# Token loads of the bonus on ScalarE's DMA queue instead of SyncE's

## The chip, the cores and the metric

One core of one Trainium2 chip. The metric is the time of one execution on the device in microseconds. The kernel before took 586.46 us, the median of three runs (584.77, 586.46 and 588.16).

A core has engines that each run their own instructions strictly in order and wait for one another by semaphores: TensorE (PE, matrix products), VectorE (DVE), ScalarE (ACT), GpSimd (POOL) and SyncE (SP). SyncE computes nothing here; it issues transfers between DRAM and on-chip memory. ScalarE can issue transfers too, from a queue of its own, but an issue is then an instruction among its computations: while ScalarE issues, or waits to issue, its next copy doesn't start.

## The reference

A recurrent attention block feeds a two-layer network. For each of 4 batches and 8 heads, with 768 tokens and 48 channels per head:

```python
for t in range(S):
    cur = einsum('bhd,bhe->bhde', u[None] * kt, vt)
    y[:, :, t] = einsum('bhd,bhde->bhe', rt, state + cur)
    state = wt[:, :, :, None] * state + einsum('bhd,bhe->bhde', kt, vt)
```

The 3072 outputs of 384 channels then go through the network:

```python
h = x @ w_in                        # 384 -> 2048
g = h * (1.0 / (1.0 + np.exp(-h)))  # silu
return g @ w_out                    # 2048 -> 384
```

The term with `u` is the bonus: a token sees itself with the weight `u` in place of the state's decay.

## The kernel before

**Tiling.** The tokens are worked through in 12 units: 6 stretches of 128 tokens, each for two pairs of batches (`units`). In a unit the recurrence is written as a matrix of scores between tokens, built level by level (blocks of 2, 4, ... 64 tokens), where VectorE and GpSimd multiply decays into queries and keys and TensorE forms the products. Scores times values gives the attention's output.

**Staging.** `mix(i)` is the list of steps of unit i's attention. It is a list of groups, and each group comes with a number: so many steps of the network are issued behind it. These steps belong to earlier units: `downs(i - 2)`, the second layer of unit i-2 in 7 steps, then `ups(i - 1)`, the first layer of unit i-1. From unit 3 on the first layer has 20 steps (`first_part`): each is a group of products on TensorE, and between them ScalarE and VectorE copy, join and activate partial sums that stand in four banks. TensorE can go on with a bank only when such a copy or join (L1161 and L1164 on ScalarE, L1167 on VectorE) is done with it. The order is written out by hand: what is issued earlier in this list stands earlier on its engine.

**The bonus from unit 4 on.** `load_rk(i)` loads unit i's r, k and w as tokens (384 KB each) into `tokens_rk` and `tokens_w`, 16 tokens of one head to a row. There is one buffer of each, so a load has to wait until GpSimd has read the unit before. GpSimd makes products from them: `block_bonus(i, 0)` to `(i, 3)` (L490) at the end of unit i-1's mix, and steps 4 to 7 in unit i's own. `tokens_w` is read last in step 5, `tokens_rk` in step 7. VectorE sums the products into `block_sums` (`block_sum`, L527). The sums stand by head and block and are wanted by token, so `block_move` sends them through DRAM: one store to `kept` (L549), and when it has landed, five reads into `spare` (one at L554, four at L556). VectorE turns them (`block_turn`, L560) and writes them into the scores (`block_write`, L566).

**Around the change.** SyncE issues nearly everything, in program order: the blocks of w, k and r for the next unit (L127), its values v (L140, L147), the output stores (L1297), then the r and k tokens (L158), the store of the sums, the w tokens, and the five reads. ScalarE issues only the passage of the attention's output through DRAM (`x_out` L930, `x_in` L936). Behind the group with `block_move` stand, in VectorE's order, joins of the first layer, then `block_turn`, the first half of `block_write`, another join (L1167) and the second half. Each transfer also waits for the one that used the same completion counter before it; there are eight counters in rotation over both queues, in the program's order.

`sum_steps(i, 3)` and `sum_steps(i, 4)` are the last two parts of the sums; `keep_level` and `go_on` belong to the scores; `in_weight_sum` makes sums of weights once, in unit 4. `ahead` is true while there is a next unit, so the token loads stand in mix(4) to mix(10).

Of the kernel before, what the change touches and what calls it, by code (L numbers as in the profile page):

```python
# [38 lines left out]
def kernel(  # L39
# [11 lines left out]
    nc = tc.nc  # L51
# [56 lines left out]
    def load_twos(to, src, i, queues):  # L108
        n, b0 = units[i]
        for b in range(NB):  # L110
            queues[b].dma_start(out=to[b * L // 2:(b + 1) * L // 2],
                                in_=src[b0 + b, :, n * L:(n + 1) * L, :].rearrange("h (i s) d -> i h (s d)", s=2))
# [33 lines left out]
            t1 = t0 + L - (g + 1) * 32  # L146
            nc.sync.dma_start(out=vq[i][g * 32:(g + 1) * 32], in_=v[b0 + 1, :, t1:t1 + 32, :].rearrange("h t d -> t h d"))  # L147

    def load_rk(i, parts=range(3)):

        if i < NPAIR:
            for x, src in enumerate((r, k)):
                load_twos(tokens_rk[:, x].rearrange("p h s d -> p h (s d)"), src, i, [nc.sync] * NB)
            return
        n, b0 = units[i]
        for x in parts:
            to, src = ((tokens_rk[:, 0], r), (tokens_rk[:, 1], k), (tokens_w, w))[x]
            nc.sync.dma_start(out=to.rearrange("p h s d -> p (h s d)"),  # L158
                              in_=src[b0:b0 + NB, :, n * L:(n + 1) * L, :].rearrange("b h (i s) d -> (b h) i (s d)", s=2 * BLK))


# [294 lines left out]
    at = 768  # L456
# [486 lines left out]
    def both(fn, i, *args):  # L943
        return [(fn, i, b, *args) for b in range(NB)]

    def block_loads(i, names="wkr"):
        return [(load_blocks, i, name, g) for name in names for g in range(4)]

    def mix(i):

        ahead = i + 1 < len(units)

        def at(now, *steps):
            return steps if now else ()

        def bonus_steps(j, *steps):
            return [(block_bonus, j, x) for x in steps]

        def sum_steps(j, *steps):
            return [(block_sum, j, x) for x in steps]  # L960

        def turns(j):
            return [*both(turn, j, "w"), (product, j, 0), *both(turn, j, "k")]

        def start(j):
            return [*[(product, j, l) for l in range(1, NL)], (grow_own, j, 1)]

        end = [[*at(ahead, *bonus_steps(i + 1, 0, 1, 2, 3))],
               [*at(i < len(units) - NB, (turn_apart, i), (turn_k, i)), (y_state, i), *both(y_values, i), *at(ahead, *turns(i + 1)), *at(ahead and i > NFAST, *sum_steps(i + 1, 0, 1)),
                *at(i <= NFAST, (sums, i - 1, FH // 2 - 2)), *both(update, i), *at(not ahead, (move_x, i))]]  # L970
        if i < NPAIR:
            groups = [[*both(turn, i, "w"), (product, i, 0)],
                      [*both(turn, i, "k"), (odd_ones, i)], [*both(turn, i, "r"), (start_levels, i), (prepare_keys, i, 1)],
                      [(prepare, i, 1), *[(product, i, l) for l in range(1, NL)]],
                      [(burst, i, 1), (keep_level, i, 1)],
                      [(keep_level, i, 2), (go_on, i, 2)],
                      [(prepare, i, 3), (reverse_v, i), (bonus, i, 0), (bonus_sum, i, 0)],
                      [(bonus, i, 1), (burst, i, 3), (keep_level, i, 3), (bonus, i, 2)],
                      [(keep_level, i, 4), (go_on, i, 4), (bonus_sum, i, 1), (load_rk, i + 1), (load_u,)],
                      [(prepare, i, 5), (make_block_mask,), (bonus_spread, i)],  # L980
                      [(burst, i, 5), (keep_level, i, 5, 0), (keep_level, i, 6, 0), (go_on, i, 6), (bonus_write, i, (0,)), (keep_level, i, 5, 1), (keep_level, i, 6, 1), (bonus_write, i, (1,))], *end]
            groups = list(zip(groups, (1, 1, 0, 2, 1, 1, 1, 1, 1, 2, 2, 1, 1)))
        else:
            j = i - 1
            groups = [([*both(turn, i, "r"), (grow_own, i, 0), (x_out, j)], 2),
                      ([*start(i), *bonus_steps(i, 4), (x_in, j), (reverse_v, i)], 1),
                      ([(grow_queries, i, 2), (sums_of_x, j, 0)], 1),
                      ([(odd_keys, i, 2), (grow_keys, i, 2, False), (sums_of_x, j, 1)], 1),
                      ([(sums_of_x, j, 2), *sum_steps(i, 2), (prepare, i, 3), *bonus_steps(i, 5, 6, 7), (sums_of_x, j, 3, 4, 5, 6)], 2),
                      ([(burst, i, 3), (keep_level, i, 3)], 2),  # L990
                      ([*sum_steps(i, 3)], 1),
                      ([], 1),
                      ([*at(ahead, (load_rk, i + 1, (0, 1))), *sum_steps(i, 4), (block_move, i, False), *at(ahead, (load_rk, i + 1, (2,))), (block_move, i, True), (keep_level, i, 4)], 2),
                      ([(go_on, i, 4)], 1),
                      ([], 2),
                      ([], 1),
                      ([(sums_of_x, j, 7)], 1),
                      ([(prepare, i, 5)], 2),
                      ([], 1),
                      ([(burst, i, 5), (keep_level, i, 5, 0), (keep_level, i, 6, 0), (go_on, i, 6), (block_turn, i), (block_write, i, 1)], 2),  # L1000
                      ([(keep_level, i, 5, 1), (keep_level, i, 6, 1)], 1),
                      ([(block_write, i, 0)], 1),
                      (end[0], 2), (end[1], 0)]

        if i == NPAIR:
            groups[0][0][:0] = sum_steps(i, 0, 1)
        loads = [*at(i >= NPAIR and ahead, *block_loads(i + 1, "wk")), *at(i >= NPAIR - 1 and ahead, *block_loads(i + 1, "r"))]
        if i + 1 < len(units):
            loads.insert(len(loads) // 2, (load_values, i + 1))

        if i < NPAIR:
            behind = [group for group, _ in groups[8:]]
            for at, group in enumerate(behind):
                group += loads[at * len(loads) // len(behind):(at + 1) * len(loads) // len(behind)]
        elif ahead:
            blocks = block_loads(i + 1, "wkr")
            for at, some in ((0, blocks[0:3]), (1, blocks[3:6]), (2, [*blocks[6:8]]), (3, [(load_values, i + 1)]),
                             (9, blocks[8:9]), (10, blocks[9:10]), (11, blocks[10:11]), (12, blocks[11:])):
                groups[at][0].extend(some)
        return groups  # L1020
# [278 lines left out]
    def ups(i):  # L1299

        if i >= NFAST:
            made = [[(first_part, i, n)] for n in ORDER]
            if i == len(units) - 1:
                made[10].append((sums_of_x, i, 7))
            made[17].append((sums, i, 0))
            made[-1].append((sums, i, 1))
            return made
        steps = [[(up, i, m)] for m in range(FC // 2)]
        for m in range(FH // 2 - (1 if i == len(units) - 1 else 2)):

            steps[FH // 2 + 1 + m].append((sums, i, m))
        steps[-1].append((sums, i, FH // 2 - 1))
        return steps

    def downs(i):
        return [[(quarter, i, x)] for x in range(7)]
# [73 lines left out]
    for i in range(3, len(units)):  # L1390
        steps = downs(i - 2) + ups(i - 1)
        groups = mix(i)
        if i == NTOK + 1:
            groups[4][0].insert(1, (weight_sums, 3))
            for place, engine, names in ((4, nc.vector, ("m",)), (5, nc.vector, ("n",)), (6, nc.vector, ("m1", "m2")), (7, nc.gpsimd, ("q14", "q3")),
                                         (8, nc.vector, ("q12a", "q12")), (11, nc.gpsimd, ("q", "n13", "t"))):
                groups[place][0].append((in_weight_sum, engine, *names))
        if i == NFAST + 1:
            keep_banks()
            for place, engine, names in ((4, nc.vector, ("u1",)), (5, nc.vector, ("u",)), (7, nc.vector, ("q19",)), (5, nc.gpsimd, ("q7",)),  # L1400
                                         (8, nc.gpsimd, ("q8", "q1")), (9, nc.gpsimd, ("q5", "q9")), (13, nc.gpsimd, ("q6", "q17"))):
                groups[place][0].append((in_weight_sum, engine, *names))
        for group, count in groups:
            do(*group)
            for step in steps[:count]:
                do(*step)
            steps = steps[count:]
# [34 lines left out]
```

## Time and profile before

| | |
|---|---|
| Median of the runs | 586.46 us |
| The profiled execution | 587.88 us |
| Its span in the profile | 586.0 us |
| TensorE busy | 564.1 us (96%) |
| VectorE busy | 470.4 us (80%) |
| GpSimd busy | 385.3 us (66%) |
| ScalarE busy | 259.6 us (44%) |
| Granted TensorE clock, mean | 0.985 |
| SyncE's queue (q1) | 49.52 MB, 42.0% of the 16 DMA engines' time |
| ScalarE's queue (q10) | 6.88 MB, 4.6% |

How to read the profile: the span runs from the first to the last recorded instruction; the execution's own time lies a little over it. Busy time is the sum of an engine's computing instructions; issues of transfers are not counted in it and stand as SPq (SyncE's) or ACTq (ScalarE's). A line of a timeline gives the start in us from the span's start, the length, the engine, the source line, what is written and read, and in brackets how long the engine was idle before and what ended that. The chain is the work that ended last, followed back from the end; `DMA kept<-block_sums` in it is the time from issue to landing of that transfer. PEclk is the share of full clock that TensorE was granted.

### The profile page before, as it was taken

To read this page: it belongs to the slowest core of one execution; us is meant where nothing else is said; L and a number is where in the kernel's file an instruction comes from. 1 tells how busy PE (TensorE), PEld (TensorE's weight loads), DVE (VectorE), ACT (ScalarE), POOL (GpSimd) and SP (SyncE) were. 2 spreads that over 40 slices of the span, in tenths; PEclk is the share of its full clock that TensorE was granted. 3 is DMA by queue.
4 is the path that set the end of the run, shared out by engine and by line. 5 is a ranking of instruction groups with operands and counts; after the bars stand their busy time and mean duration, and the time that the engine had idled before them with its cause. 6 is when DMAs were issued, how large, how long until landed. Compare 5 with 4: busy or idle time off the path is not lost.

```text
span 586.0 us, 18814 instructions
## 1 busy us (share of the span) xinstructions
PE 564.1 (96%) x7782; PEld 523.5 (89%) x7782; DVE 470.4 (80%) x748; ACT 259.6 (44%) x556; POOL 385.3 (66%) x459
## 2 busy tenths in 40 slices
PE   8989999999999899979999989999999989999997
PEld 7768876798899899969999979999989989999997
DVE  7979789898899999767799879689889879682350
ACT  5679694431531561442372352263263253372330
POOL 6989778457799988747776856765975964810000
PEclk9989999999999999989999998999999999999999
DMA  9957785443445634635634545554455453102000
GB/s 226 314 118 217 161 238 83 48 93 91 95 83 88 134 53 69 151 39 92 138 54 85 113 81 89 103 93 80 81 114 94 88 107 67 34 8 55 29 3 26
DMA packets 206485, 57.59 MB, mean 98 GB/s; under 512 B 186048, under 2 KB 198208, under 8 KB 206400
## 3 DMA queue, kind: packets, MB, share of 16 engines
q1 hardware_dynamic: 198288, 49.52, 42.0%
q10 hardware_dynamic: 8112, 6.88, 4.6%
q8 instruction: 61, 1.00, 0.7%
q14 instruction: 24, 0.20, 0.1%
HBM read 47.14 MB, written 9.18 MB: 96 GB/s over the span
## 4 chain that ended last, share of the span: by engine, by line
PE 47%; DMA 5%; SPq 3%; issue 1%; DVE 1%; POOL 1%; ACT 0%; DVEq 0%
PE p_o L1283 22%; PE p_o L1140 9%; PE p_h L1140 6%; PE p_h L1283 4%; DMA kept<-block_sums 3%; PE p_m L861 2%; DMA spare<-kept 2%; SPq L556 2%; PE p_m L840 2%; PE p_sc L697 1%; PE p_m L697 1%; SPq L158 1%; PE p_sc L906 1%; POOL ruk L490 1%; PE p_sc L816 1%
## 5 line engine op out<-in xcount | busy, mean ns | idle before, releaser
L639 POOL TENSOR_TENSOR tk<-tk,tw 128x256 f32<-128x256 f32 x128 | 96.0, 770 | 45.0 <-ACT tk L609 29.0
L1283 PE MATMUL p_o<-own,temps 128*128 128x192 f32 x528 | 88.1, 326 | 0.2 <-DVE temps L1254 0.2
L1283 PEld LDWEIGHTS p_o<-own,temps 128*128 128x128 f32 x528 | 86.0, 190 | 0.5 <-DVE temps L1254 0.5
L1140 PE MATMUL p_o<-xt,w_in_sb 128*64 128x128 f32 x1152 | 73.9, 274 | 11.1 <-DVE p_o L1167 9.4
L407 POOL TENSOR_TENSOR tw<-tw 128x256 f32<-128x256 f32 (+6 forms) x83 | 41.7, 502 | 55.9 <-DVE tw L361 52.0
L1140 PEld LDWEIGHTS p_o<-xt,w_in_sb 128*64 128x64 f32 x1152 | 64.9, 137 | 12.9 <-DVE p_o L1167 10.8
L1033 PE MATMUL p_h<-xt,w_in_sb 128*128 128x256 f32 x288 | 67.8, 391 | 0.8 <-POOL w_in_sb L260 0.6
L1033 PEld LDWEIGHTS p_h<-xt,w_in_sb 128*128 128x128 f32 x288 | 54.7, 194 | 9.4 <-POOL w_in_sb L260 1.1
L1283 PE MATMUL p_o<-w_out_sb,gt 128*128 128x192 f32 x340 | 60.0, 329 | 1.6 <-DVE ob L1291 0.9
L1283 PEld LDWEIGHTS p_o<-w_out_sb,gt 128*128 128x128 f32 x340 | 55.3, 190 | 2.8 <-DVE ob L1291 1.2
L490 POOL TENSOR_TENSOR ruk<-tokens_rk 128x384 f32<-128x384 f32 x48 | 53.0, 1126 | 4.6 <-DMA tokens_rk<-in_k_dram 4.0
L621 DVE TENSOR_TENSOR tr<-tr,tw 128x512 f32<-128x512 f32 x61 | 54.2, 889 | 0.5
L1288 ACT COPY partial<-p_o 128x192 f32<-128x192 f32 x33 | 10.5, 319 | 93.8 <-PE p_o L1283 80.3
L609 ACT COPY tk<-tk 128x256 f32<-128x256 f32 x52 | 20.9, 402 | 54.8 <-POOL tk L639 40.7
L1254 DVE TENSOR_TENSOR temps<-gt 128x512 f32<-128x512 f32 (+1 forms) x48 | 38.4, 838 | 0.0
L1164 ACT ACTIVATE gt<-p_o 128x512 f32<-128x512 f32 x45 | 26.0, 601 | 24.7 <-PE p_o L1140 24.7
L715 DVE COPY_PREDICATED score<-mask,p_sc 128x512 f32<-128x512 int8 x42 | 31.3, 801 | 3.5 <-PE p_sc L697 3.3
L1283 PE MATMUL p_o<-w_out_sb,temps 128*128 128x192 f32 x176 | 30.4, 326 | 0.0
L797 ACT COPY score<-p_sc 32x128 f32<-32x128 f32 x80 | 20.5, 257 | 20.2 <-DVE score L566 18.2
L1283 PE MATMUL p_h<-w_out_sb,gt 128*128 128x192 f32 x168 | 29.1, 326 | 0.0
L1283 PEld LDWEIGHTS p_o<-w_out_sb,temps 128*128 128x128 f32 x176 | 28.9, 190 | 0.0
L490 POOL TENSOR_TENSOR spare<-tokens_rk 128x384 f32<-128x384 f32 x24 | 28.2, 1188 | 0.6
(239 smaller groups left out, 1273.0 us busy)
## 6 DMA issues: line engine op xcount, KB each, us to landing
w_out_sb<-in_moe_w_in_dram SPq DMA_DIRECT2D x6, 768.0 KB, 7.1
w_out_sb<-in_moe_w_out_dram SPq DMA_DIRECT2D x4, 768.0 KB, 6.7
own<-in_moe_w_out_dram SPq DMA_DIRECT2D x4, 768.0 KB, 5.9
tokens_rk<-in_r_dram SPq DMA_DIRECT2D x8, 384.0 KB, 4.6
tokens_rk<-in_k_dram SPq DMA_DIRECT2D x8, 384.0 KB, 5.4
tokens_w<-in_w_dram SPq DMA_DIRECT2D x8, 384.0 KB, 5.4
turned<-yt ACTq DMA_DIRECT2D x16, 192.0 KB, 2.7
xt<-turned ACTq DMA_DIRECT2D x8, 384.0 KB, 3.8
```

Of the source, the lines that this page charges most:

```text
L407: engine.tensor_tensor(out=up, in0=t[:, :, 0::2], in1=t[:, :, 1::2], op=ALU.mult)
L490: mul = lambda out, one, two: nc.gpsimd.tensor_tensor(out=out, in0=one, in1=two, op=ALU.mult)
L609: nc.scalar.copy(out=keys(i, X[(l + 1) % 2] * L + c, [4 * c, blocks], [c, 2], [1, c]), in_=keys(i, NP * L + c, [4 * c, blocks], [NP * L + ...
L621: nc.vector.tensor_tensor(out=odd, in0=odd, in1=tw[i][l][:, :, 0::2][:, :, :, None].to_broadcast([128, Q, L >> (l + 1), c]), op=ALU.mult)
L639: nc.gpsimd.tensor_tensor(out=out, in0=have, in1=odd_products(i, l, b, *blocks), op=ALU.mult)
L715: nc.vector.copy_predicated(out=dst, mask=masks[l][:, :, None].to_broadcast([128, NB, NP, ni, c]), data=sc[e].rearrange("p (b q) (i c) -> ...
L797: nc.scalar.copy(out=score[x * c:(x + 1) * c, i % NSC, e, b * NP:(b + 1) * NP, (first + 1) * c:(first + 2) * c], in_=made[i, l][e][x * c:( ...
L1033: nc.tensor.matmul(p_h[:, a, :], lhsT=w_in_sb[:, c, f * 128:(f + 1) * 128], rhs=xt[i][:, c, :], start=(a == 0 and c == 0), stop=(a == 1 an ...
L1140: nc.tensor.matmul(p[h:h + PD, q, :], lhsT=left[:, f:f + PD], rhs=right, start=first and q == 0, stop=q == 3, skip_group_check=True)
L1164: nc.scalar.activation(out=g(f, t), in_=have, func=AF.Silu)
L1254: nc.vector.tensor_tensor(out=out, in0=one, in1=two, op=op)
L1283: nc.tensor.matmul(p, lhsT=left(f), rhs=right[:, f, :], start=which in (0, 1, 3) and f == 0, stop=f == FH - 1, skip_group_check=True)
```

## The change

The r, k and w tokens of the next unit are issued from ScalarE's queue in place of SyncE's, in mix(4) to mix(10). `load_rk` takes the queue as an argument. The w load is taken out of `block_move`'s middle and put one group ahead, in a group that was empty; the r and k loads are taken out of the head of the same group and put three groups later: the empty group of two steps behind `go_on` is cut into two of one step each, and they stand in the second. The numbers of steps behind the groups are the same in sum. As there is one group more, the weight sums that were put into group 13 go into group 14, the same place as before. Block loads that are put into groups by number (9 to 12) stand one step of the network earlier for two of the r blocks.

In the built programs the order on TensorE, VectorE and GpSimd is the same in both. SyncE has 21 issues fewer. ScalarE has 21 more, at two places in each of the seven mixes: w behind the second of two copies at L1161 and ahead of an activation (L1164); r and k behind an activation at L1183 and ahead of a copy at L1161.

```diff
-    def load_rk(i, parts=range(3)):
+    def load_rk(i, parts=range(3), queue=nc.sync):
...
-            nc.sync.dma_start(out=to.rearrange("p h s d -> p (h s d)"),
+            queue.dma_start(out=to.rearrange("p h s d -> p (h s d)"),
                               in_=src[b0:b0 + NB, :, n * L:(n + 1) * L, :].rearrange("b h (i s) d -> (b h) i (s d)", s=2 * BLK))
...
                       ([*sum_steps(i, 3)], 1),
+                      ([*at(ahead, (load_rk, i + 1, (2,), nc.scalar))], 1),
+                      ([*sum_steps(i, 4), (block_move, i, False), (block_move, i, True), (keep_level, i, 4)], 2),
+                      ([(go_on, i, 4)], 1),
                       ([], 1),
-                      ([*at(ahead, (load_rk, i + 1, (0, 1))), *sum_steps(i, 4), (block_move, i, False), *at(ahead, (load_rk, i + 1, (2,))), (block_move, i, True), (keep_level, i, 4)], 2),
-                      ([(go_on, i, 4)], 1),
-                      ([], 2),
+                      ([*at(ahead, (load_rk, i + 1, (0, 1), nc.scalar))], 1),
                       ([], 1),
                       ([(sums_of_x, j, 7)], 1),
...
-                                         (8, nc.gpsimd, ("q8", "q1")), (9, nc.gpsimd, ("q5", "q9")), (13, nc.gpsimd, ("q6", "q17"))):
+                                         (8, nc.gpsimd, ("q8", "q1")), (9, nc.gpsimd, ("q5", "q9")), (14, nc.gpsimd, ("q6", "q17"))):
```

## The prediction

> **What bounds the kernel now.** I read the page's chain first, then the busy time by stage, then the chain in order of time at one stage, then the SyncE, ScalarE and VectorE rows there. Times written as +x are us after TensorE starts the level-3 scores (L697) of a unit; that start is the left edge of each window below, from mix(5) to mix(10).
>
> ```profile
> PE 47%; DMA 5%; SPq 3%; issue 1%; DVE 1%; POOL 1%; ACT 0%; DVEq 0%
> PE p_o L1283 22%; PE p_o L1140 9%; PE p_h L1140 6%; PE p_h L1283 4%; DMA kept<-block_sums 3%; PE p_m L861 2%; DMA spare<-kept 2%; SPq L556 2%; PE p_m L840 2%; PE p_sc L697 1%; PE p_m L697 1%; SPq L158 1%; PE p_sc L906 1%; POOL ruk L490 1%; PE p_sc L816 1%
> ```
>
> TensorE carries the chain, but the trip of the bonus through DRAM (`kept`, then back into `spare`) and its issues stand in it too. By stage:
>
> ```profile
> core 0: us, PE busy (x) PEld busy (x) DVE busy (x) ACT busy (x) POOL busy (x), PEclk, DMA share, GB/s
> 234.90:284.13 49.23, 45.52 (x660) 43.85 (x662) 37.43 (x64) 18.25 (x42) 33.17 (x45) 0.93 0.50 91
> 284.13:326.76 42.63, 42.63 (x693) 41.53 (x695) 37.97 (x59) 18.60 (x43) 29.25 (x35) 1.00 0.48 92
> 326.76:375.43 48.67, 45.75 (x692) 44.47 (x695) 38.15 (x63) 18.65 (x43) 32.93 (x45) 0.93 0.49 89
> 375.43:418.05 42.62, 42.62 (x692) 41.52 (x695) 37.96 (x59) 18.60 (x43) 29.24 (x35) 1.00 0.50 94
> 418.05:461.70 43.65, 42.65 (x693) 41.52 (x694) 38.42 (x63) 18.59 (x43) 32.36 (x41) 1.00 0.51 96
> 461.70:505.09 43.39, 41.55 (x645) 40.37 (x647) 34.62 (x59) 17.99 (x41) 30.71 (x39) 1.00 0.39 80
> ```
>
> Mixes 6 and 8 are gapless: 42.6 us, TensorE busy throughout. Mixes 5 and 7 do the same work in 49.23 and 48.67 and lose clock (0.93); mixes 9 and 10 lose 1.00 and 1.84. The chain in order of time inside mix(7):
>
> ```profile
> 334.81 5.08 DMA kept<-block_sums
> 339.91 0.38 SPq L554
> ...
> 342.73 3.31 DMA spare<-kept
> 346.20 0.24 DVE spare L560
> ...
> 348.01 0.70 DVE p_o L1167
> 348.76 1.09 PE p_o L1140 x16
> ```
>
> Store, five reads back, `block_turn` on VectorE, and behind that wait on the same engine the join of the first layer (L1167), for which TensorE stands still: 3.64, 2.92, 1.00 and 1.84 us in mixes 5, 7, 9, 10. After the two longest the clock is down for a while; after the two short ones it is not:
>
> ```profile
> 299.00:310.00 11.00, 11.00 (x232) 1.00 0.28 42
> 348.00:359.00 11.00, 10.24 (x156) 0.69 0.39 63
> 438.00:449.00 11.00, 10.87 (x179) 1.00 0.46 72
> ```
>
> Why the store takes long: in mix(7) it is issued right behind 768 KB of r and k on the same queue (issues at 333.53, 334.13, store at 334.81) and lands after 5.08; in mix(11), with no token loads, the same store takes 1.55:
>
> ```profile
> 511.52 0.33 SPq L549 DMA_DIRECT2D kept<-block_sums  x1
> 513.07 0.38 SPq L554 DMA_DIRECT2D spare<-kept  x1
> ```
>
> **The change, part by part.** Seven mixes (4 to 10) are touched, 21 loads; mix(11) has none, and units up to 4 are still loaded by SyncE.
>
> *Removed from SyncE.* r (0.55) and k (0.59) ahead of the store, w (0.54) behind it. Sums stand ready at 242.29, 333.93, 425.22 and 468.11 in mixes 5, 7, 9, 10; SyncE is past its two output stores at 242.84, 333.44, 423.96, 467.32. So the store is issued at about 242.90, 333.95, 425.24, 468.13 in place of 244.22, 334.81, 426.21, 468.70: 1.32, 0.86, 0.97 and 0.57 sooner. Its landing was 5.9, 5.1, 4.5 and 5.0. Bounds now: 1.5 (mix 11, no load near) to 5.9. I take 2.3, mix(8)'s, where the store came 3.1 us after k's issue: the w load will stand 2.1 us before it and is half as large. The store then lands near +9.5.
>
> *Added on ScalarE.* An issue occupies the queue in order. Its places in mix(9):
>
> ```profile
> 421.96 0.59 ACT L1161 COPY gt<-p_o 128x512 f32<-128x512 f32 x1 [0.29 <-PE p_o L1140]
> 424.58 0.60 ACT L1164 ACTIVATE gt<-p_o 128x512 f32<-128x512 f32 x1 [2.03 <-PE p_o L1140]
> ...
> 426.33 0.60 ACT L1183 ACTIVATE gt<-p_h 128x512 f32<-128x512 f32 x1 [0.26 <-PE p_h L1140]
> 428.13 0.59 ACT L1161 COPY gt<-p_o 128x512 f32<-128x512 f32 x1 [1.21 <-PE p_o L1140]
> ```
>
> w goes into the 2.03 us hole (0.54 of it): free. r and k (1.14 and some 0.05 between) go into the 1.21 hole: 0 to 0.1 late. If issues run to SyncE's longest, 0.92 and 1.27, the copy behind is 1.0 late; its result is wanted by the join at 429.55 and its bank by the matmuls at 429.50, 0.8 after it now ends. I take 0; upper bound 0.2 x 7 = 1.4 us. What could hold these issues: GpSimd's last reading (w: done 420.24; r and k: 424.22, issue at 426.95), and in the built program a load eight places earlier that shares a completion counter: for w a late k block (issued by 418, landing in 1.9 to 3.5), for r and k loads of v issued by 422.98, landing in 2.7. All are done at least 1 us before.
>
> *The reads back.* Five issues, then a landing: 5.1 us (mix 9) to 6.3 (mix 7), so the blocks are in at +14.6 to +15.8. VectorE comes to them at +16.35 in mixes 7, 9 and 10. But r and k now fly from +8.9 on, beside the reads. Bound from below 0; from above 3.6, what r and k did to the store (5.08 against 1.55). Nearest: mix(8), where w went out 1.9 us before the first read, and the reads' landings were 2.8 to 3.8 against 1.9 to 3.0 in mix(9): 0.9 from 384 KB. For twice as much I take 1.8 at the front, less for the last read, which is issued near +12.6: some 1.0. So +15.6 to +16.8: VectorE waits 0 to 0.45, and TensorE's stall was 0.1 to 0.8 less than that wait in three of four mixes. I put 0.4 us of stall to each of mixes 5 to 10, bounds 0 and 2.
>
> *Moved later: tokens for GpSimd.* k lands 4.2 to 6.1 after its issue near +9.5, so at +13.7 to +15.6; GpSimd starts the next unit's products at +13.84 (431.89). It slips up to 1.8 us. Cover: after those products it waits 9.39, 5.77, 9.35, 5.77, 6.38, 7.57 us for VectorE's `tw` (mixes 5 to 10). Free; without that cover it would cost 1.8 per unit. SyncE reaches its r blocks up to 3.4 us earlier and then waits for VectorE as before.
>
> *Sum.* Stall and lost clock over the gapless length: 49.23 - 42.63 = 6.6; 48.67 - 42.63 = 6.0; 1.0; 1.84: 15.5 us. Less 6 x 0.4 = 2.4: 13.1. That the gapless pace holds from mix to mix is read from mix(9), which follows a gapless one: its sums were ready only 0.8 us later than mix(8)'s. The profiled execution took 587.88 (span 586.0 and 1.88 around it), 1.42 over the median of 586.46. 587.88 - 13.1 = 574.8; as a median, 573.4.
>
> **Rivals.** *Only the issue time is saved.* The reads lose beside r and k what the store wins. Then the stalls shrink by 1.32 + 0.86 + 0.97 + 0.57 = 3.7: 582.7. Stalls of 2.3 and 2.1 remain in mixes 5 and 7, between 1.84, which kept the clock, and 2.92, which did not; if the clock holds, 3.0 + 3.1 more come back: 576.6. For it: r and k fly at the time of the reads. Against it: the last read goes out 3 us after k. The Trainium skill has this as a rule (DMA: Bandwidth & Descriptors, "Issuing engines are not separate DMA queues"): loads started by ScalarE and SyncE run on the same 16 engines and interleave, so a second issuer saves issue time only. By it the time is 582.7 to 576.6; but here the loads also move in time, away from the store, which the rule leaves open. On the clock the Trainium skill (TensorE: Matmul & The Clock Gate, "What's actually happening") halves it after about 3.4 us idle, by which stalls of 2.3 and 2.1 would keep it and the time be 576.6; mix(7)'s 2.92 was already enough, so the trace is less kind.
>
> *Slower: the reads are hit as the store was.* If r and k cost the last read 3.6, it lands at +18.2 to +19.4, VectorE waits 1.9 to 3.0 in mixes 5 to 10, and near 2.9 a stall costs 6.0 with its clock. Six times 6.0 less 15.5 is +20.5: 607. It decides from 15.5 / 6 = 2.6 us lost per mix, so about where the clock starts to fall. Against it: in mix(6) w went out 2.1 us before the reads and they landed in 1.8 to 2.5, not slowed at all.
>
> *Same: the stall is replaced.* ScalarE's copy comes late by two long issues, or a wait of r or k for the loads of v runs over; 15.5 / 7 = 2.2 us per mix would cancel the gain. The v loads would have to land 3 us later.
>
> **How the numbers follow.** As computed (570 to 577): 0.55. Issue time only (577 to 583): 0.24. Replaced, within 0.5% (583.5 to 589.4, about what a measurement of this kernel can tell from no change): 0.08. Slower: 0.13. The first two end faster: 0.79. The range runs from all 15.5 us won, 586.46 - 15.5 = 571.0 less half the runs' spread (1.7), so 569.3, to the end of the issue-only case, 583: 0.79 of the chances.
>
> **What would show it.** Right: three loads per unit at L158 on ScalarE's queue, 0.54 to 0.6 us each; store to landing below 3 us in mixes 5, 7, 9, 10; TensorE's idle time ahead of L1140 for L1167 from 11.1 us to 3 or less; clock 1.00 in the stages that had 0.93; GpSimd waiting for `tokens_rk` up to 1.8 us per mix. Wrong: VectorE still waiting over 2 us at L560 for `spare<-kept`, a copy at L1161 late behind its issues, or a GpSimd that reaches `tw` after VectorE.

## The result and the profile after

The changed kernel takes 580.26 us (median of five runs, 579.7 to 581.95) against 586.46 (five runs, 584.77 to 588.16): a ratio of 0.9895, 95% interval 0.9867 to 0.9923. It is faster by 6.2 us. The forecast was 13.1: its sign was right and its range holds the time, but it was more than twice the gain. The profiled execution took 580.03 (span 578.1, mean clock 1.000 in place of 0.985).

The page's chain of the changed kernel is followed back over only 12% of the span, nearly all of it TensorE. That stretch lies behind mix 10, the last one that was changed, so the view says nothing of the change. (Below the change, line numbers are higher by one than in the kernel before: the join is L1168, the copy L1162, the first layer L1141.) The busy time by stage does say something. The windows run from the first level-3 scores of mixes 5 to 10 to those of the next unit, here in the changed kernel:

```profile
core 0: us, PE busy (x) PEld busy (x) DVE busy (x) ACT busy (x) POOL busy (x), PEclk, DMA share, GB/s
234.66:278.53 43.87, 43.11 (x690) 41.59 (x689) 39.24 (x62) 18.64 (x44) 32.35 (x41) 1.00 0.53 96
278.53:323.97 45.44, 43.23 (x689) 41.57 (x689) 38.87 (x63) 18.53 (x43) 32.58 (x41) 1.00 0.53 94
323.97:366.67 42.70, 42.66 (x689) 41.52 (x689) 38.08 (x60) 18.61 (x43) 31.67 (x39) 1.00 0.51 95
366.67:410.21 43.54, 43.25 (x690) 41.58 (x689) 39.21 (x62) 18.54 (x43) 32.35 (x40) 1.00 0.52 97
410.21:454.76 44.55, 43.25 (x690) 41.57 (x689) 39.05 (x63) 18.54 (x43) 32.79 (x41) 1.00 0.51 94
454.76:496.34 41.58, 41.54 (x641) 40.36 (x641) 35.45 (x57) 17.78 (x41) 30.13 (x36) 1.00 0.42 85
sum 261.68, PE 257.03 PEld 248.20 DVE 229.90 ACT 110.62 POOL 191.87; mean PE 42.84 PEld 41.37 DVE 38.32 ACT 18.44 POOL 31.98
```

and mix 5 and the sum over the same six mixes in the kernel before:

```profile
233.93:284.06 50.13, 46.18 (x689) 44.38 (x688) 38.33 (x65) 18.68 (x44) 34.07 (x47) 0.93 0.50 90
...
sum 271.09, PE 261.38 PEld 253.78 DVE 225.52 ACT 111.11 POOL 188.56; mean PE 43.56 PEld 42.30 DVE 37.59 ACT 18.52 POOL 31.43
```

The two long mixes are gone (43.87 and 42.70 in place of 50.13 and 48.67), and so is the lost clock. But mixes 6 and 8, gapless before at 42.6, now take 45.44 and 43.54, and mix 9 takes 0.9 more than it did. The six mixes give back 9.4 us; the time up to mix 5 and that behind mix 10 are 0.7 and 0.8 longer, which leaves 7.9 between the two spans. The profiled execution of before lay 1.42 above its median, the new one 0.23 below, which makes 6.2 of it.

The waits of the changed kernel (us in total, times, longest):

```profile
ACT gt L1162 <- DMA out_dram<-temps: 8.0, 3, 3.0
DVE spare L560 <- DMA spare<-kept: 7.0, 6, 2.2
PEld p_o L1141 <- DVE p_o L1168: 5.8, 11, 1.6
...
PEld p_o L1141 <- ACT gt L1162: 2.1, 3, 1.1
```

Before, VectorE waited at L560 for 10.7 us in four mixes, and TensorE 11.1 us for the join. Now VectorE waits 7.0 in all six, and there is a wait that did not exist: ScalarE's copy, three times, 2.4 to 3.0 us, each time behind a token load that could not be issued. Before, ScalarE stood idle for 1.2 us ahead of the same copy anyway, until TensorE was done, so the copy comes 1.2 to 1.9 us late. In mix 8, ScalarE's rows of the changed kernel (start, length, engine, line; in brackets the idle time before and what ended it):

```profile
375.53 0.54 ACTq L158 DMA_DIRECT2D tokens_rk<-in_r_dram  x1
377.84 0.54 ACTq L158 DMA_DIRECT2D tokens_rk<-in_k_dram  x1
378.48 0.59 ACT L1162 COPY gt<-p_o 128x512 f32<-128x512 f32 x1 [2.44 <-DMA out_dram<-temps]
```

and SyncE's in the same mix:

```profile
374.89 0.41 SPq L549 DMA_DIRECT2D kept<-block_sums  x1
378.85 0.38 SPq L554 DMA_DIRECT2D spare<-kept  x1
```

r goes out, k waits 1.77 us, and the copy starts 3.03 us after the activation ahead of it (L1184, at 375.45). Before, this distance was 1.80 (in mix 9, 426.33 to 428.13), so the copy is 1.2 late. The store took 3.96 us from issue to the first read, where in the kernel before this mix had 2.31.

### The profile page after: what moved, and what is told of

Read it like the earlier page. It is cut to its first block, busy times and chain, and to the rows that moved or that the text cites. A ratio compares the mean times of both kernels' runs of the same rounds, so it can differ in the third digit from the quotient of the medians.

```text
span 578.1 us, 18816 instructions
## 1 busy us (share of the span) xinstructions
PE 559.5 (97%) x7782; PEld 517.7 (90%) x7782; DVE 477.9 (83%) x748; ACT 259.2 (45%) x556; POOL 389.3 (67%) x459
## 3 DMA queue, kind: packets, MB, share of 16 engines
q10 hardware_dynamic: 11136, 15.14, 10.1%
## 5 line engine op out<-in xcount | busy, mean ns | idle before, releaser
L639 POOL TENSOR_TENSOR tk<-tk,tw 128x256 f32<-128x256 f32 x128 | 94.6, 759 | 36.2 <-ACT tk L609 28.6
L1141 PE MATMUL p_o<-xt,w_in_sb 128*64 128x128 f32 x1152 | 73.6, 274 | 5.8 <-DVE p_o L1168 2.7
L1141 PEld LDWEIGHTS p_o<-xt,w_in_sb 128*64 128x64 f32 x1152 | 64.3, 137 | 8.4 <-DVE p_o L1168 4.3
L1034 PE MATMUL p_h<-xt,w_in_sb 128*128 128x256 f32 x288 | 66.1, 384 | 1.8 <-POOL w_in_sb L260 1.6
L621 DVE TENSOR_TENSOR tr<-tr,tw 128x512 f32<-128x512 f32 x61 | 50.5, 829 | 0.5
L1255 DVE TENSOR_TENSOR temps<-gt 128x512 f32<-128x512 f32 (+1 forms) x48 | 44.1, 956 | 0.0
L648 POOL TENSOR_TENSOR tk<-tk,tw 128x256 f32<-128x256 f32 x32 | 28.1, 898 | 0.0
```

What stands on the lines that cost most here:

```text
L621: nc.vector.tensor_tensor(out=odd, in0=odd, in1=tw[i][l][:, :, 0::2][:, :, :, None].to_broadcast([128, Q, L >> (l + 1), c]), op=ALU.mult)
L639: nc.gpsimd.tensor_tensor(out=out, in0=have, in1=odd_products(i, l, b, *blocks), op=ALU.mult)
L648: nc.gpsimd.tensor_tensor(out=have, in0=have, in1=odd_products(i, l, b, [2, NP * ni]), op=ALU.mult)
L1034: nc.tensor.matmul(p_h[:, a, :], lhsT=w_in_sb[:, c, f * 128:(f + 1) * 128], rhs=xt[i][:, c, :], start=(a == 0 and c == 0), stop=(a == 1 an ...
L1141: nc.tensor.matmul(p[h:h + PD, q, :], lhsT=left[:, f:f + PD], rhs=right, start=first and q == 0, stop=q == 3, skip_group_check=True)
L1255: nc.vector.tensor_tensor(out=out, in0=one, in1=two, op=op)
```

## The experiments

Three theories were on record. A: what is left is traffic, the tokens' bytes beside the small transfers. B: the gapless pace isn't reached anyway, so 15.5 us were never there. C: ScalarE's issues and their waits cost the time. Each ratio is to the kernel before on the same chip.

**e1: no token loads.** From the changed kernel, mixes 4 to 10:

```diff
-                      ([*at(ahead, (load_rk, i + 1, (2,), nc.scalar))], 1),
+                      ([], 1),
...
-                      ([*at(ahead, (load_rk, i + 1, (0, 1), nc.scalar))], 1),
+                      ([], 1),
```

> The changed kernel without the 21 token loads of mixes 4 to 10 (the bonus of units 5 to 11 is computed from old tokens, all else is as before). Theory A (traffic): the token loads slow the transfers that fly beside them, and that is all that is left to win. Then every mix from 5 to 10 takes 41.6 to 42.8 us, VectorE never waits at L560 for the reads, and the time is 571 to 573. Theory B (pace): the gapless 42.6 us of mixes 6 and 8 were a gift of the slow mixes before them, GpSimd can't hold them, and without any token load the time stays at 577 or above, with GpSimd late at the sums.

Measured: 572.38 us against 587.76, ratio 0.9726 (0.9667 to 0.9784). By stage, mix 8 and the sum over the six mixes:

```profile
362.55:405.17 42.62, 42.62 (x690) 41.52 (x689) 38.91 (x61) 18.61 (x43) 32.02 (x40) 1.00 0.43 72
...
sum 255.47, PE 255.09 PEld 248.06 DVE 231.68 ACT 111.08 POOL 192.17; mean PE 42.52 PEld 41.34 DVE 38.61 ACT 18.51 POOL 32.03
```

Mixes 6 to 10 are gapless, and VectorE never waits at L560. (Mix 5 takes 43.49, more than the 42.8 that was expected.) B falls: 15.4 us were to be had, and the loads are the cause of all of it. The changed kernel's mixes are 261.68 - 255.47 = 6.2 us above this.

**e2: w left out. e3: r and k left out.** One of the two lines above is emptied, the other stays.

> The changed kernel without the 7 loads of w (steps 3 and 5 of the bonus use old w). Theory A: w flies beside the loads of v; without it v lands in 3 us or less, so neither the store nor the issues of r and k have to wait for v's completion counters, the store lands in 2.5 us or less, but the reads back stay at 4 us beside r and k. VectorE still waits 0.2 to 1 us per mix; 575 to 577. Theory C (ScalarE held): all that matters is that ScalarE is held by its issues of r and k (0.84 + 0.23 + 0.28 us of TensorE's time); 578.9, and the store lands as late as with w.

> The changed kernel without the 14 loads of r and k (the bonus of units 5 to 11 is computed from old r and k). Theory A: the reads back land in 2 to 3 us in place of 4 to 5, VectorE's wait at L560 (7.0 us in all) goes to under 1.5, the store stays at 2.5 to 4.4; 573 to 576. Theory C: only ScalarE's being held goes, 1.4 us: 578.9, and the reads stay at 4 us.

Measured: e2 577.67, ratio 0.9809 (0.9747 to 0.9872); e3 574.21, ratio 0.9748 (0.9677 to 0.9819). e3 is in A's range. e2 lies between A's 575 to 577 and C's 578.9, so its time decides nothing; that its store lands in 1.9 us, and not as late as with w, is A's. The landings (KB each, median us from issue to landing, mixes 5 to 11, of those that the trace records; each trace lacks some; the 32 KB row is the first read, the 8 KB row the four behind it), first in the kernel before:

```profile
vq<-in_v_dram SPq DMA_DIRECT2D x24, 48.0 KB, 2.5
kept<-block_sums SPq DMA_DIRECT2D x7, 64.0 KB, 4.8
spare<-kept SPq DMA_DIRECT2D x27, 8.0 KB, 2.8
spare<-kept SPq DMA_DIRECT2D x7, 32.0 KB, 2.6
```

the changed kernel:

```profile
vq<-in_v_dram SPq DMA_DIRECT2D x24, 48.0 KB, 4.4
kept<-block_sums SPq DMA_DIRECT2D x7, 64.0 KB, 3.6
spare<-kept SPq DMA_DIRECT2D x28, 8.0 KB, 3.9
spare<-kept SPq DMA_DIRECT2D x7, 32.0 KB, 4.4
```

e2, without w:

```profile
vq<-in_v_dram SPq DMA_DIRECT2D x24, 48.0 KB, 2.4
kept<-block_sums SPq DMA_DIRECT2D x7, 64.0 KB, 1.9
spare<-kept SPq DMA_DIRECT2D x28, 8.0 KB, 4.8
spare<-kept SPq DMA_DIRECT2D x7, 32.0 KB, 5.1
```

e3, without r and k:

```profile
vq<-in_v_dram SPq DMA_DIRECT2D x24, 48.0 KB, 4.1
kept<-block_sums SPq DMA_DIRECT2D x7, 64.0 KB, 3.6
spare<-kept SPq DMA_DIRECT2D x28, 8.0 KB, 2.7
spare<-kept SPq DMA_DIRECT2D x7, 32.0 KB, 2.4
```

The two loads do two separate things. w, moved ahead, flies beside the v loads and the store: 2.4 to 4.4 and 1.9 to 3.6. r and k fly beside the reads: 2.4 to 4.4 or more for the first, 2.7 to 3.9 or more for the others. With w gone ScalarE is no longer held at its copy (no such wait in e2), so C's wait is a consequence of w's traffic: the loads of v land later, and what stands behind them in the rotation of completion counters can't be issued. The waits view names `out_dram<-temps` as the releaser; the built program puts a load of v eight places ahead of k. The two land at about the same time, and no run tells which it was. SyncE is held in the same way: in mixes 5 and 6 its own waits show 0.5 and 1.6 us at the store (L549) for `vt<-in_v_dram`, another load of v, and the store goes out 1.5 and 2.0 us after the sums are ready.

Why bytes matter so much is read from the share of the 16 DMA engines' time (next to last column). The store's flight and the reads' flight in mix 7 of the kernel before:

```profile
336.50:339.90 3.40, 3.40 (x68) 3.40 (x64) 2.97 (x6) 2.11 (x5) 0.46 (x1) 1.00 1.03 268
339.91:344.00 4.09, 4.09 (x120) 3.85 (x118) 2.76 (x3) 3.31 (x9) 4.09 (x6) 1.00 0.30 25
```

and in mix 8 of the changed kernel:

```profile
374.89:378.85 3.96, 3.96 (x74) 3.76 (x70) 3.96 (x7) 1.26 (x3) 1.22 (x3) 1.00 1.05 301
378.85:382.67 3.82, 3.59 (x108) 3.31 (x108) 2.92 (x6) 3.52 (x10) 1.41 (x2) 1.00 0.78 137
```

In both of the stretches in which the store flies beside tokens the share is above 1, on whichever queue the tokens were issued, and the reads' stretch went from 0.30 to 0.78. That the small transfers are slow because the engines are full is read from these shares; that bytes are what counts is tested in e7.

**e4: all three behind the reads, on SyncE.** From the kernel before:

```diff
-  ([*at(ahead, (load_rk, i + 1, (0, 1))), *sum_steps(i, 4), (block_move, i, False), *at(ahead, (load_rk, i + 1, (2,))), (block_move, i, True), (keep_level, i, 4)], 2),
+  ([*sum_steps(i, 4), (block_move, i, False), (block_move, i, True), *at(ahead, (load_rk, i + 1)), (keep_level, i, 4)], 2),
```

> The kernel before with r, k and w issued by SyncE behind the five reads back, so that nothing of them is in flight before. Theory A: store 1.5 to 2.5 us, reads 2 to 3 us, no wait at L560; GpSimd gets r and k at about +18.5 in place of +13.8 and has 5.8 us to spare before VectorE's tw, so 571 to 574, better than the changed kernel. Rival: GpSimd's slip of 4.7 us eats its slack, tw's products come late and the level products with them; then 580 or more.

Measured: 581.61, ratio 0.9876 (0.9816 to 0.9936). The trip was undisturbed: no wait at L560. But A's figure for the time failed and its rival's held: k is in only near +20, GpSimd's products start there in place of +13.9, and mixes 6 to 9 take 44.3 each. GpSimd has a deadline, and it lies before +20, although its wait for `tw` behind the products (up to 3.2 us here) still looks like time to spare.

**e5: store first, tokens second, on SyncE.** From the kernel before; ScalarE's queue isn't used:

```diff
-  ([*at(ahead, (load_rk, i + 1, (0, 1))), *sum_steps(i, 4), (block_move, i, False), *at(ahead, (load_rk, i + 1, (2,))), (block_move, i, True), (keep_level, i, 4)], 2),
+  ([*sum_steps(i, 4), (block_move, i, False), *at(ahead, (load_rk, i + 1, (0, 1))), (block_move, i, True), *at(ahead, (load_rk, i + 1, (2,))), (keep_level, i, 4)], 2),
```

> The kernel before with one order changed on SyncE's queue: in each of mixes 4 to 10 the store of the sums goes out first, then r and k, then the five reads, then w. Nothing goes to ScalarE's queue. All work is done. Times are +x us after TensorE starts the level-3 scores of a unit. Theory A (what the tokens cost is their traffic beside the small transfers, so only the moment counts, not the queue): the store lands in 1.5 to 2 us with nothing ahead of it, so near +8 to +9, the v loads keep their 2.0 to 2.5 us, ScalarE is never held; r and k fly beside the reads and slow them to 4 to 5 us, as in the changed kernel. That leaves reads in at about +14 to +16 and a stall of at most 1 us in some mixes: 573 to 578. Theory D (a queue works its transfers off in order, so reads behind 768 KB on the same queue wait for all of it, which on ScalarE's queue they do not): the reads land 5 us or more after their issue, as r and k do themselves (4.5 to 5.1), VectorE waits over 2 us for the blocks in most mixes, and the time is 580 or more.

Measured: 575.35 (575.16 to 575.64) against 588.21, ratio 0.9781 (0.9766 to 0.9796). It beats both kernels. SyncE's rows in mix 7:

```profile
329.44 0.33 SPq L549 DMA_DIRECT2D kept<-block_sums  x1
329.86 0.54 SPq L158 DMA_DIRECT2D tokens_rk<-in_r_dram  x1
330.45 0.60 SPq L158 DMA_DIRECT2D tokens_rk<-in_k_dram  x1
331.14 0.54 SPq L554 DMA_DIRECT2D spare<-kept  x1
```

The store went out 0.42 us ahead of the same 768 KB that in the kernel before stood ahead of it, and it took 1.70 us in place of 5.10. (Over mixes 5 to 10 of e5 it takes 1.7 to 2.1, except in mix 6, with 3.6; there it takes 3.3 without any token load, in e1.) What comes first seems to be through before the engines are full. VectorE's wait at L560 is 3.2 us in all, over three mixes. D, a queue that works its transfers off in order, has neither its wait (over 2 us in most mixes) nor its time (580 or more), although the one first read whose landing is recorded in the mixes took 5.5.

**e6: w behind the reads on SyncE, r and k as changed.**

```diff
-  ([*at(ahead, (load_rk, i + 1, (2,), nc.scalar))], 1),
-  ([*sum_steps(i, 4), (block_move, i, False), (block_move, i, True), (keep_level, i, 4)], 2),
+  ([], 1),
+  ([*sum_steps(i, 4), (block_move, i, False), (block_move, i, True), *at(ahead, (load_rk, i + 1, (2,))), (keep_level, i, 4)], 2),
```

> The changed kernel with one part undone: r and k stay on ScalarE's queue at the new place, w goes out on SyncE behind the five reads. All work is done. Theory A: w no longer flies beside the v loads and the store (v loads back to about 2.0 us, store 1.5 to 2, ScalarE no longer held), the reads still fly beside r and k (4 to 5 us): as with the w loads left out, 577 to 578. If w in this place still disturbs something, it would be the reads (it is issued behind them and could only add to r and k): over 579.

Measured: 577.49, ratio 0.9835 (0.98 to 0.987), as A has it: within e2's interval, with w loaded. Beside the changed kernel (0.9895) the early w costs some 3.5 us. e5 and e6 issue r and k at nearly the same moment (e5 at +7.7 to +10.0, e6 at +8.4 to +9.8), one from SyncE, the other from ScalarE. ScalarE's queue shows no advantage; if there is a difference, it favours SyncE (575.35 against 577.49 on one chip).

**e7: half of r and k, no w.** The two loads on ScalarE cover one batch of the pair:

```diff
-            queue.dma_start(out=to.rearrange("p h s d -> p (h s d)"),
-                              in_=src[b0:b0 + NB, :, n * L:(n + 1) * L, :].rearrange(...))
+            nb = 1 if queue is nc.scalar else NB
+            queue.dma_start(out=to.rearrange("p h s d -> p (h s d)")[0:nb * 64],
+                              in_=src[b0:b0 + nb, :, n * L:(n + 1) * L, :].rearrange(...))
```

> The changed kernel with the w loads of mixes 4 to 10 left out and the r and k loads of these mixes cut to the rows of the first batch of the pair, half of the bytes each (2 x 192 KB). Left out of the computation: the bonus of units 5 to 11 uses stale w, and stale r and k for the second batch. The issues on ScalarE stay two in number. Without any token load the time was 572.4, with r and k whole and without w 577.7. Theory A (bytes beside the reads): the reads' landing is some halfway between 2.0 and 4.8 us, VectorE waits under 1.5 us for the blocks, and the time is 573.5 to 576. Theory C (the issues and their waits on ScalarE): the same two issues in the same place cost the same, 577 to 578.

Measured: 572.88, ratio 0.9738 (0.9718 to 0.9757): as fast as with no loads, a little under A's 573.5 to 576, and far from C's 577 to 578. The same two issues at the same place cost nothing when they carry half the bytes. Why all of it went and not half isn't settled: the trace of this run records the landing of only two first reads, and those (5.2 and 5.4) are not shorter than in e2; the later reads are (3.9 in the median against 4.8). VectorE's waits at L560 are 0.46 and 0.21 in two mixes, so the last read was mostly in by the time VectorE came. By stage, the sum over the six mixes:

```profile
sum 255.33, PE 254.85 PEld 248.10 DVE 231.04 ACT 111.23 POOL 194.84; mean PE 42.47 PEld 41.35 DVE 38.51 ACT 18.54 POOL 32.47
```

**e8: the other queue, the old place.** r, k and w from ScalarE where the kernel before has them:

```diff
-  ([*at(ahead, (load_rk, i + 1, (0, 1))), *sum_steps(i, 4), (block_move, i, False), *at(ahead, (load_rk, i + 1, (2,))), (block_move, i, True), (keep_level, i, 4)], 2),
+  ([*at(ahead, (load_rk, i + 1, (0, 1), nc.scalar)), *sum_steps(i, 4), (block_move, i, False), *at(ahead, (load_rk, i + 1, (2,), nc.scalar)), (block_move, i, True), (keep_level, i, 4)], 2),
```

> Only the queue is changed, not the place: r, k and w are issued by ScalarE where the kernel before has them, ahead of the sums and inside the move. All work is done. In ScalarE's order all three then stand ahead of the activation of the first layer near +6.5, and r and k must wait for GpSimd's last reading of the tokens near +6.2. Theory A: r and k fly at the time of the store as in the kernel before, so the store still lands in 4 to 5 us where the sums come right behind; ScalarE adds three issues (1.7 us) behind +6.2, so its activation is about 1.4 us late and TensorE stands for that in each mix: 586 to 594. If it is the queue that counts and not the moment, the store lands below 3 us and the time is below 582.

Measured: 587.55, ratio 0.9987 (0.9961 to 1.0012): no difference, in A's range. ScalarE's lateness cost less than expected (TensorE waits 2.3 us for its copies, in four mixes). The store in mix 5, with SyncE's queue free of tokens:

```profile
242.60 0.60 SPq L549 DMA_DIRECT2D kept<-block_sums  x1
250.01 0.38 SPq L554 DMA_DIRECT2D spare<-kept  x1
```

7.41 us, longer than the 5.91 of before; here w too went out ahead of the store (r, k and w at 241.17, 241.75 and 242.41). The queue alone gains nothing that can be measured; all of the change's gain is the moment.

**e9: r ahead of the reads, k and w behind them, on SyncE.**

```diff
-  ([*at(ahead, (load_rk, i + 1, (0, 1))), *sum_steps(i, 4), (block_move, i, False), *at(ahead, (load_rk, i + 1, (2,))), (block_move, i, True), (keep_level, i, 4)], 2),
+  ([*sum_steps(i, 4), (block_move, i, False), *at(ahead, (load_rk, i + 1, (0,))), (block_move, i, True), *at(ahead, (load_rk, i + 1, (1, 2))), (keep_level, i, 4)], 2),
```

> The kernel before with another order on SyncE's queue in mixes 4 to 10: the store of the sums, then r, then the five reads, then k and w. Nothing goes to ScalarE's queue. All work is done. With r and k both ahead of the reads it took 575.4, with no token loads 572.4, with r, k and w all behind the reads 581.6 (there k was in only near +20 and GpSimd's products came too late). Theory A (bytes beside the reads, and a deadline for GpSimd): only r flies beside the reads, 384 KB in place of 768, so VectorE waits at most 0.5 us for the blocks; k goes out near +12 and is in near +17 to +18, 3 us later than before, and GpSimd has 5.2 us of waiting for tw behind its products: 572.5 to 575. If GpSimd's slip is not covered, TensorE waits for the scores' products (L639) or VectorE for the outputs as in the kernel with all three behind the reads, and the time is 576 to 581.

Measured: 581.35, ratio 0.9899 (0.9844 to 0.9955). A's traffic half held: VectorE never waits at L560. The time lies at the end of the rival's 576 to 581, and A's deadline was wrong: GpSimd starts near +18.6 and mixes 7 to 9 take 44.0, though it still waits 3.77 us for `tw` behind its products. GpSimd's row in mix 8 (the releaser in brackets is the step that ended last by the profile; in mixes 7 and 10 the same wait is put down to k's load):

```profile
384.85 3.01 POOL L490 TENSOR_TENSOR ruk<-tokens_rk 128x384 f32<-128x384 f32 x2 [3.79 <-DVE score L566]
```

VectorE's rows there, sums of the network's second layer, with no idle time between them:

```profile
386.93 2.89 DVE L1254 TENSOR_TENSOR temps<-gt 128x512 f32<-128x512 f32 x2
389.75 1.49 DVE L1254 TENSOR_TENSOR temps<-temps,gt 128x512 f32<-128x512 f32 x1
391.34 1.31 DVE L1254 TENSOR_TENSOR temps<-gt,temps 128x512 f32<-128x512 f32 x1
392.57 2.10 DVE L1254 TENSOR_TENSOR temps<-gt 128x512 f32<-128x512 f32 x2
```

and the same instructions in e1:

```profile
382.92 2.90 DVE L1255 TENSOR_TENSOR temps<-gt 128x512 f32<-128x512 f32 x2
385.74 0.68 DVE L1255 TENSOR_TENSOR temps<-temps,gt 128x512 f32<-128x512 f32 x1
386.52 0.69 DVE L1255 TENSOR_TENSOR temps<-gt,temps 128x512 f32<-128x512 f32 x1
387.13 1.29 DVE L1255 TENSOR_TENSOR temps<-gt 128x512 f32<-128x512 f32 x2
```

0.81, 0.62 and 0.81 longer: GpSimd's products now run beside these instructions, and VectorE comes 2.2 us later to all that follows. It has little reserve there (39.5 to 40 of 44 us busy), and TensorE's weight loads wait for it at the outputs (L1291): 3.8 us over the six mixes, where e1 has no such wait. That this is the whole of the 1.4 us by which mixes 7 to 9 are longer is not shown.

## Why the prediction was right in sign and wrong in size

*Sum of the stalls, 15.5 us.* Right: e1 has 15.4. But the window of mix 5 was opened 0.97 us behind that mix's first level-3 scores (234.90, the scores start at 233.93), and its gapless length is not 42.63 but 43.49 (e1). By luck the two errors cancel: 50.13 - 43.49 = 6.64, where the sum has 6.6.

*Issues on ScalarE, cost 0.* The three loads per unit stand there as forecast, 0.54 to 0.61 us each, and in e2 they fit into the holes, but for one that took 1.55. Wrong was the sentence on what could hold them, that the loads of v are all done 1 us before. They landed in 4.4 us in place of 2.5, because of the w load that the same change puts beside them. That held k's issue in mixes 6, 8 and 9; the copy behind it came 1.2 to 1.9 us late, and TensorE waited 0.84, 0.23 and 0.28 for it: 1.35 in all, just under the upper bound of 1.4.

*The store and the reads: blocks in at +15.6 to +16.8.* This is the step that failed. They were in at +16.2 to +19.2. VectorE came at +15.5 to +17.0, as forecast (+16.35), and so waited 0.6 to 2.2 us per mix in place of 0 to 0.45. The lateness is that of the store. It was to land near +9.5; it landed at +9.9 to +12.9. It went out at +7.3 in mixes 7 and 10, about as forecast (+7.2), and up to +10.1 elsewhere: in mixes 5 and 6 it was held for the load of v, and the sums of mixes 6, 8 and 9 are ready only at +8.0 (e1 has them at +7.2 in mixes 6 to 10, where before it was +6.5 or +7.2). Then it took 1.8 to 4.4 us, where 2.3 was forecast. The 2.3 came from a store 3.1 us behind k; what w alone does was underrated (3.6 in the median with w, in the changed kernel as in e3; 1.9 without, in e2).

*The reads back, 0.4 us of stall per mix, 2.4 in all.* The reads themselves were priced well for the changed kernel: from the first read's issue to the last block 4.8 to 6.3 us, where the prediction has 6.1 to 7.3 (from +9.5 to +15.6 and +16.8). Their medians rose by 1.8 for the first and 1.1 for the others, where it has 1.8 and 1.0. But that goes with a late store, behind which less of r and k is still in flight. With the store at 1.9 us, in e2, the reads' medians are 5.1 and 4.8, in e1 2.2 and 2.2, so 2.9 and 2.6 longer. The two legs hang together, and the prediction priced them apart. (Its upper bound for the reads, 5.08 - 1.55, is 3.5 and not 3.6.)

What the term cost: TensorE's mixes stand 6.2 us above e1's in place of 2.4, and the stretch behind mix 10 is 0.95 longer. The bounds, 0 and 2 per mix, hold five of the six mixes (0.1 to 1.9); mix 6 lost 2.8. Against e1's ratio, r and k alone cost 4.9 us (e2), twice the term; w alone costs 1.3 (e3, whose trace has the loss in mix 5, 46.94 us; mixes 6 to 9 are gapless at 42.6, their later store notwithstanding); both together 9.9. So 3.7 us appear only where both are there, as the held issue of k does: w delays what k waits for, and the store. The prediction saw the first of these three, at half its size. (The ratios leave 2 to 4 us of play; the two profiled spans, 578.1 and 570.1, are 8.0 apart.)

*GpSimd's slip.* Forecast up to 1.8, hidden by its wait for `tw`. It slipped 1.1 to 3.3 (products at +15.0 to +17.2). The cover is smaller than was read: e4 and e9 show that a GpSimd later by 4.0 to 5.9 us (mixes 6 to 10) costs while that wait is still 2.7 us (e4, in the mean) and 3.8 us (e9); in e9 the way is through VectorE. At the smaller slip of the changed kernel that price is not seen: its six mixes' L1255 instructions take 44.9 us of VectorE, in e1 41.7, but in e7 they take 47.1 (there L1256), and e7's mixes are as short as e1's (255.33 and 255.47). What the slip does move is the sums: in e5 the products start at +14.2 in mix 7 and at +14.7 in mix 8, and the next sums are ready at +7.2 and +8.0.

*The rival.* "Only the issue time is saved" gave 576.6 to 582.7, and the time is inside it. Its account doesn't fit all the same: it left 2.3 and 2.1 us in mixes 5 and 7, which lost 0.4 and 0.1 against e1, while mixes 6, 8 and 9 lost 2.8, 0.9 and 1.9. The rule beside it in the Trainium skill (DMA: Bandwidth & Descriptors, "Issuing engines are not separate DMA queues") is borne out by e8 (0.9987) and by e5 against e6. What the rule leaves open, the moment, is worth 12.9 us in e5 (588.21 to 575.35). The clock kept 1.00 in the changed kernel, whose longest stall was 1.31 us; so nothing in it tests the rival's condition on the clock.

## What to carry to other kernels

When a transfer is moved to another queue, price the moment and not the queue: list the small, awaited transfers that will now fly beside it, and charge them at the rate of the stretch where the DMA engines are already full. The cheapest order tried here that loads everything puts the small awaited transfer first and the bulk right behind it, on one queue (e5). And price a chain of awaited transfers as one: what the first wins by going early, the next can lose beside the same bytes. An engine's wait behind a step is no proof of slack: look at what that engine runs beside once it is later.

## What the runs showed of the hardware

A store of 64 KB issued 0.42 us ahead of 768 KB lands in 1.7 us (e5, mix 7); behind the same bytes it takes 5.1 in the kernel before, and bytes on another queue slow it too (7.41 in e8, behind 1152 KB). Order of issue counts here within half a microsecond.

VectorE's two-input instructions on 128x512 f32 take 0.68 us alone (e1) and 1.3 to 1.5 beside GpSimd's products (e9): one engine slows another without a wait in any row. The Trainium skill says of this (SBUF — State Buffer, "Who interferes with whom") that a VectorE instruction with two inputs in on-chip memory contends with a GpSimd instruction that reads there, and that the later one blocks. These rows agree that the VectorE instruction takes longer; which of the two came later they don't show.
